# New order tables for eleven stretches of a zipformer block on one Trainium2 core

## The chip, the cores and the metric

The kernel runs on one core of a Trainium2 chip. The metric is device microseconds of one execution; the median of the runs is compared. The core has five engines that take their instructions in the order written: TensorE (PE), ScalarE (ACT), VectorE (DVE), GpSimd (POOL) and SyncE (SP, which here only issues DMAs).

## What is computed

The reference is one conformer-like block over x of shape (2, 4000, 144) in bfloat16, with 4 heads of 36:

```
x = x + 0.5 * (silu(ln(x) @ w_ff1a) @ w_ff1b)
q, k, v = heads(ln(x) @ w_qkv)
x = x + softmax(q @ k.T * 36**-0.5) @ v @ w_o
a, b = split(ln(x) @ w_pw1);  h = a * sigmoid(b)
x = x + silu(depthwise_conv5(h)) @ w_pw2
x = x + 0.5 * (silu(ln(x) @ w_ff2a) @ w_ff2b)
out = ln(x)
```

Attention is over all 4000 positions of a batch, so its exponentials (2 x 4 x 4000 x 4000) are the bulk of the work.

## The kernel before, in words

The 8000 tokens are 16 chunks of 500. A chunk goes through feed-forward 1, the projections to Q, K and V, attention, convolution and feed-forward 2; the chunks' parts overlap. Attention of one chunk runs over 63 key tiles of 64 keys, which makes 1008 *attention tiles* in all. An attention tile n is: score matmuls into two PSUM banks (`PS<-QT,KT`), an exponential into a buffer of PT, and product matmuls (`PS<-PT,VA`) that add into two PSUM banks kept for the sums. There are 11 PT buffers and 6 PSUM banks for all else.

The exponential has several forms, chosen for each tile by one letter of TYPES:

- A: ACT takes the whole tile, 128x1000, in one `ACTIVATE PT<-PS`; R is the half tile at the end of the keys.
- D: DVE makes it from bits: two `TENSOR_SCALAR PT<-PS` of 128x500 (called z0 and z1), then on PT y (`TENSOR_SCALAR`), m (`TENSOR_TENSOR`) and w (`TENSOR_SCALAR`), each 128x1000. Both m and w go into product matmuls, so that such a tile has twice as many.
- W: as D, with one z of 128x1000.

PAIRS lists attention tiles that share y, m and w as one instruction each over 2x1000 elements (`ymw_args`, L2024; `settle`, L2167).

The program is first recorded by a planner with costs (`Rec.op`, L350; `Sched`). Then `Rec.choose` (L413) puts each small flexible operation (a PSUM copy, a residual, the steps of a layernorm) on DVE, POOL or ACT by a letter of UNITS: d, p or a. `settle` rebuilds the attention tiles from TYPES, BANKS (PSUM banks of each tile) and SLOTS (PT buffers), and `Rec.arrange` (L467) orders the blocks of instructions of every engine by the table ORDER, which holds two characters for each block. The waits on semaphores are worked out after that (`finish`, L537), so the order on each engine is wholly in the tables. Every instruction is issued from one line, L591, so that groups are told apart by their tiles.

Names that the prediction uses: XN is the normalised token block of a layernorm and ST its statistics (`BN_STATS`, on DVE); RS holds the scale, made on POOL by a `TENSOR_SCALAR` and a power (`TENSOR_TENSOR`), after which four `XN<-X,RS` are written (POOL, or DVE as `XN<-X,ST,RS`) (`ln`, L1238). An SP `DMA_TRANSPOSE` then turns XN into XTB (`dma_transp`, L1216), the input of the next matmuls. The K projection is copied from PSUM into KT (`proj`, L1506). A residual (`residual`, L1360) is a DVE `SCALAR_TENSOR_TENSOR X<-PS,X`, or on ACT a copy `X<-PS`, for which PE adds x first by two matmuls `PS<-X,EYE`. U holds the convolution's input, whose edges POOL copies (`halo`, L1701).

Of the kernel before, what the change touches and what calls it, by code (L numbers as in the profile page):

```python
# [13 lines left out]
H = 4  # L14
# [38 lines left out]
        '1]1M1O1V1^1L1*1S1a1-1N1g1h1b1=141l1k#a1v1u1o1[1,1+1z1y#b2!1}1p1e1i1x1E2-2,2%1`1{1|1_21202$1w1Z1f2#2&'  # L53
        '2425#c2>232?1m1j282C2/2B1n1c1q1d#d2F29222G1s1r2Q2P2E2*2+2@262K2A2D2J2U2T2)2.2H1t2X2Y2I#e2(2^2W2]2b2['
        '2a2;2:#f272e2`2S2l2f2<2V2m2N#g2i2r3#2R2s2g2=2w2L2v2M2_2Z2h2c2O3!2d2{2z2k2j3)3*#i3-3.#j2p2q3132#h3536'
        '2y3+3/2x3:393B3A302n342|3=3>372}332o3G383H#k3K3L3,3S3?3%2u3O3P3$3;3T2t3@3I3Z3Y3F3N3M3&3<3_3^3f#l3J3C'
        '3c3[3b3g3m3l3(3Q3a3D3`3R3x3W3X3p3q#m3u3t3]3d3E4(3e3n3j3o3r4#3V4!3U3s4&473y#n#o4-4.3h3i4$3k4%414B4A3v'
        '483w4>4=#p#q#r4I4J4E4F4D4)424/4?40#s4+4,4M4N#t#u4Q4@4C4R4G4L4H4;4V4U4*4O#w#v4a4`3}4K4P494Y4e4d4:#x4h'
        '4i4<3|4T4S4Z4W4s4r454X4m4f4g3z4w4v4l4643444b3{4{4z#y#z5#4t5!5-4u4j5.4}4y4[4x4k4c4|5&52515(4]5$4q4p55'
        '56#{5=5%595:4_4o4^5D5C5>5350574n545/5X5W5<5G5+585N5M#|5F5`5;5H5Q5,5Y5Z5[5]5E5B5O5*5a5)#}5A5P5d5e5^5_'  # L60
        '5?5R5@5i5h$!5m5l$#5q5p5t5f5g6!5}5j5J5b5c5k5I5w6&6%5L5r5o5s5K5x5n5V5U6*6+5T5S5u5v$$6/6.6962$%686(636<'
        '6=$&$(6A6@6$6#6)$)6:6E6?6D656I666;6H$*61606S6R6,6C6L675z6B6W6V$+646M6F5|6Z6G6>6[6e6Y6U5{6f6X6_6-6T6K'
        '$,$-6j6i6^6m6g6]6n6N6O6J6h5y6`6P6w6x$.6q6p6{6Q6o6|6k6l6y6r7#7$$/7(7)$0$17-7,6}6b706d767!7%77$26a717&'
        '7.7;7:6v6u7>7E6z787/7D$37H7I7*7?797<7+6c7M7L$47Q7P7G7F6s6t7T7U$5$674757X7Y7]7S$77d7c7C7J7B7^7g7K7V7h'
# [2478 lines left out]
```

## Time and profile before

| | us |
|---|---|
| median of 3 runs | 866.94 (866.67 to 867.0) |
| the profiled execution | 867.84 |
| its span in the trace | 865.7 |
| PE, ACT, DVE, POOL busy | 849.3, 835.0, 835.4, 284.8 |

The span is what the trace covers; 2.14 us of the profiled execution lie outside it. The granted clock of TensorE was full but for the ends. A busy time is that of instructions in flight: one that has been issued while the one before it finishes is counted with it, so that an engine can be short of work by a little more than its idle time. The places of the change are told by the time at which their instructions run in the trace of before.

### The profile page before, as it was taken

The numbers are of one execution on the slowest core, as the hardware profiler recorded it, in microseconds if no ns is written. First come the engines' busy times: TensorE is split into PE (matmuls) and PEld (weight loads), VectorE is DVE, ScalarE is ACT, GpSimd is POOL, SyncE is SP. The second block draws the span as 40 slices with busy tenths as digits, with TensorE's granted clock in tenths as the row PEclk, the third lists the DMA queues.
The fourth block names the chain that finished last, engine by engine and source line by source line (L and its number), as shares of the span: only waits on it lengthen the run. The fifth ranks groups of instructions, "written<-read, shape, count | busy, mean of one in ns | idle before, by whom it ended". The sixth has DMA issues, their size and how long they took to land.

```text
span 865.7 us, 27015 instructions
## 1 busy us (share of the span) xinstructions
PE 849.3 (98%) x11585; PEld 411.3 (48%) x11585; DVE 835.4 (96%) x1819; ACT 835.0 (96%) x1096; POOL 284.8 (33%) x562
## 2 busy tenths in 40 slices
PE   9999999999999999999999999999999999999996
PEld 7644434444344444444444444444444544445485
DVE  7999999999999999999999999999999999999987
ACT  6999999999999999999999999999999999999975
POOL 7771331041334301432230060230550163300854
PEclk9999999999999999999999999999999999999999
DMA  3331211102113110212210020010130021100121
GB/s 102 78 58 21 33 21 36 23 14 45 34 26 51 15 27 2 40 32 45 33 38 3 2 45 3 14 32 14 27 42 11 3 57 29 29 10 14 32 53 52
DMA packets 86330, 26.90 MB, mean 31 GB/s; under 512 B 81384, under 2 KB 86210, under 8 KB 86210
## 3 DMA queue, kind: packets, MB, share of 16 engines
q1 hardware_dynamic: 84662, 24.34, 15.4%
q8 instruction: 90, 1.47, 0.7%
q10 hardware_dynamic: 1548, 0.84, 0.4%
q14 instruction: 30, 0.25, 0.1%
HBM read 3.31 MB, written 2.30 MB: 6 GB/s over the span
## 4 chain that ended last, share of the span: by engine, by line
ACT 40%; PE 40%; DVE 16%; DMA 1%; POOL 1%; issue 0%; ACTq 0%; SPq 0%; DVEq 0%; POOLq 0%
PE PS L591 40%; ACT PT L591 37%; DVE PT L591 11%; ACT TH L591 3%; DVE ST L591 1%; DVE QT L591 1%; DVE X L591 1%; POOL XN L591 1%; DVE HT L591 1%; DVE U L591 1%; DMA XTB<-XN 1%; DMA X<-in_x_dram 0%; DMA WE<-in_w_ff1a_dram 0%; DVE KT L591 0%; ACT X L591 0%
## 5 line engine op out<-in xcount | busy, mean ns | idle before, releaser
L591 ACT ACTIVATE PT<-PS 128x1000 bf16<-128x1000 f32 (+1 forms) x793 | 729.9, 1071 | 4.9 <-PE PS L591 4.1
L591 PE MATMUL PS<-QT,KT 64*64 64x500 bf16 x3968 | 460.1, 383 | 4.3 <-ACT PT L591 1.2
L591 PE MATMUL PS<-PT,VA 64*37 64x500 bf16 x4828 | 449.7, 372 | 1.3 <-DVE QT L591 0.5
L591 DVE TENSOR_SCALAR PT<-PS 128x500 int16<-128x500 f32 x425 | 279.1, 676 | 4.4 <-PE PS L591 3.1
L591 PEld LDWEIGHTS PS<-QT,KT 64*64 64x64 bf16 x3968 | 139.8, 104 | 201.7 <-ACT PT L591 99.2
L591 PEld LDWEIGHTS PS<-PT,VA 64*37 64x37 bf16 x4828 | 163.1, 96 | 105.7 <-issue 16.4
L591 POOL TENSOR_SCALAR RS<-ST 125x4 f32<-125x4 f32 (+1 forms) x132 | 31.2, 238 | 479.3 <-DVE ST L591 475.4
L591 DVE TENSOR_SCALAR PT<-PT 128x1000 uint16<-128x1000 uint16 x430 | 172.2, 418 | 1.7 <-DVE PT L591 0.2
L591 DVE TENSOR_TENSOR PT<-PT 128x1000 bf16<-128x1000 bf16 x215 | 144.4, 676 | 0.8
L591 POOL TENSOR_SCALAR XN<-X,RS 125x144 bf16<-125x144 bf16 x246 | 141.1, 587 | 3.8 <-POOL RS L591 0.5
L591 POOL TENSOR_TENSOR RS<-RS,NHALF 125x4 f32<-125x4 f32 (+2 forms) x93 | 92.4, 998 | 50.1 <-DVE RS L591 48.0
L591 ACT ACTIVATE TH<-PS 128x500 bf16<-128x500 f32 (+3 forms) x175 | 92.7, 559 | 3.8 <-PE PS L591 3.3
L591 PE MATMUL PS<-XTB,WA 72*128 72x500 bf16 (+2 forms) x280 | 71.3, 359 | 1.1 <-DMA XTB<-XN 0.4
L591 DVE SCALAR_TENSOR_TENSOR HT<-TH,PS 128x500 bf16<-128x500 bf16 (+1 forms) x120 | 71.2, 614 | 1.1 <-ACT TH L591 0.8
L591 DVE BATCH_NORM_STATS2 ST<-X 125x6 f32<-125x288 bf16 (+1 forms) x160 | 65.6, 448 | 2.2 <-DMA X<-in_x_dram 1.6
L591 DVE SCALAR_TENSOR_TENSOR X<-PS,X 125x288 bf16<-125x288 f32 x114 | 50.7, 450 | 7.2 <-PE PS L591 6.2
L591 PE MATMUL PS<-WB,HT 128*125 128x144 bf16 (+1 forms) x640 | 52.2, 229 | 0.0
L591 PEld LDWEIGHTS PS<-WB,HT 128*125 128x125 bf16 (+1 forms) x640 | 44.9, 136 | 13.5 <-issue 3.9
L591 PEld LDWEIGHTS PS<-XTB,WA 72*128 72x128 bf16 x280 | 21.5, 97 | 29.5 <-issue 8.3
L591 PE MATMUL PS<-U,DG 128*128 128x375 bf16 (+7 forms) x204 | 28.0, 263 | 0.1
L591 POOL COPY U<-U 128x2 bf16<-128x2 bf16 (+1 forms) x54 | 10.9, 236 | 42.2 <-DVE U L591 32.0
L591 ACT ACTIVATE HT<-PS 128x500 bf16<-128x500 f32 (+3 forms) x43 | 20.6, 537 | 3.4 <-PE PS L591 2.9
(98 smaller groups left out, 523.1 us busy)
## 6 DMA issues: line engine op xcount, KB each, us to landing
X<-in_x_dram SPq DMA_DIRECT2D x16, 140.6 KB
XTQ<-XTB SPq DMA_DIRECT2D x24, 70.3 KB
out_dram<-XN SPq DMA_DIRECT2D x9, 140.6 KB
XTB<-XN SPq DMA_TRANSPOSE x53, 3.8
out_dram<-PT SPq DMA_DIRECT2D x3, 140.6 KB
out_dram<-PT ACTq DMA_DIRECT2D x2, 140.6 KB
XTB<-AN SPq DMA_TRANSPOSE x15, 3.2
WA<-in_w_ff1a_dram ACTq DMA_DIRECT2D x1, 144.0 KB
```

Of the source, the lines that this page charges most:

```text
L591: ins = getattr(eng, o.name)(*o.a, **o.k)
```

## The change

Only tables change. Between the first and the last change lie ORDER for all five engines, PLACES, TYPES (3 letters), BANKS, SLOTS, UNITS (14 letters) and PAIRS (two pairs, none before). No code is touched. The change's name says that the orders in eleven narrow stretches were searched anew off the chip, with DMA landings taken a little later than their mean; nothing of that search is in the kernel.

```diff
 TYPES = (
...
-    'AAAADAAADAAAAARDAAAADAAADAAAAADAAADAAADAAAADAAADAAADAAADWAADAAADAAAAAADAAAAAARDAADAAAAAAAADAADAAAAAA'
+    'AAAADAAADAAAAARDAAAADAAADAAAAADAAADAAADAAAADAAADAAADAAADAAADAAADAAAAAADAAAAAARDAADAAAAAAAADAADAAAAAA'
...
 UNITS = (
...
-    'daddddddddddpddppdddadaadadddpddppppddppddppddddddppdppdddppaaappdadddddppppdddadddppddppddddadddppd'
+    'ddddddddddddpdddpdddadaaddddppdddpppddppddppddddddppdppdddppaaappdadddddppppdddadddppdddpddddadddppd'
...
 PAIRS = (
+    (482, 485), (787, 790),
 )
```

What the letters come to: attention tile 356 goes from W to A, 689 from W to D, 877 from D to W. Two K copies and one residual go from ACT to DVE (at 69.2, 112.6 and 320.2 us), one residual from ACT to DVE and another from DVE to ACT (422.5 and 427.2), one from DVE to ACT (622.7); the four XN of a layernorm at 626.8 go from POOL to DVE with their sign step dropped; and of the small scale steps six go from POOL to DVE and one the other way. PE has four product matmuls fewer.

On PE the order differs in nine places, at 62.6 to 124.5 us of the trace (called A below), 175.9 to 200.2 (B), 225.7 to 252.3 (C), 262.7 to 329.3 (D), 414.0 to 452.2 (E), 562.8 to 587.6 (F), 618.5 to 675.2 (G), 685.0 to 738.5 (H) and 756.3 to 786.4 (I). Some of them hold more than one of the stretches. Outside them the orders of PE, ACT and DVE are the same, those of POOL and SP differ in a few rows between them too, and the first 62 us and last 79 us are untouched.

In place A on ACT, around 68 to 118 us: PT<-PS are exponentials, and VA, QT, KT are copies of projections. Before:

```order
L591 ACTIVATE PT<-PS 128x1000 x3
L591 ACTIVATE KT<-PS 128x500
L591 ACTIVATE PT<-PS 128x1000 x2
L591 ACTIVATE TH<-PS 128x500 x2
L591 ACTIVATE PT<-PS 128x1000 x2
L591 ACTIVATE TH<-PS 128x250
L591 ACTIVATE PT<-PS 128x1000 x36
L591 ACTIVATE VA<-PS 128x14x36
L591 ACTIVATE PT<-PS 128x1000
L591 ACTIVATE QT<-PS 128x500 x2
L591 ACTIVATE PT<-PS 128x1000 x3
L591 ACTIVATE KT<-PS 128x500
```

The same place of the change:

```order
L592 ACTIVATE PT<-PS 128x1000 x5
L592 ACTIVATE TH<-PS 128x500 x2
L592 ACTIVATE PT<-PS 128x1000 x2
L592 ACTIVATE TH<-PS 128x250
L592 ACTIVATE PT<-PS 128x1000 x36
L592 ACTIVATE VA<-PS 128x14x36
L592 ACTIVATE PT<-PS 128x1000
L592 ACTIVATE QT<-PS 128x500 x2
L592 ACTIVATE PT<-PS 128x1000 x15
```

Both KT copies are gone from ACT, and the exponentials on both sides of each follow each other. DVE does the copies as `CAST KT<-PS`.

In place E on DVE, around 425 to 432 us, with attention tiles 482 and 485. Before:

```order
L591 TENSOR_SCALAR PT<-PS 128x500 x4
L591 TENSOR_SCALAR PT<-PT 128x1000
L591 CAST VA<-PS 128x2x36
L591 TENSOR_SCALAR PT<-PT 128x1000
L591 SCALAR_TENSOR_TENSOR X<-PS,X 125x288
L591 TENSOR_TENSOR PT<-PT 128x1000
L591 CAST KT<-PS 128x500
L591 TENSOR_TENSOR PT<-PT 128x1000
L591 CAST VA<-PS 128x14x36
L591 TENSOR_SCALAR PT<-PT 128x1000
L591 CAST KT<-PS 128x500
L591 TENSOR_SCALAR PT<-PT 128x1000
```

The same place of the change:

```order
L592 TENSOR_SCALAR PT<-PS 128x500 x4
L592 TENSOR_SCALAR PT<-PT 128x2x1000
L592 CAST VA<-PS 128x2x36
L592 TENSOR_TENSOR PT<-PT 128x2x1000
L592 BN_STATS ST<-X 125x6 x2
L592 CAST KT<-PS 128x500
L592 CAST VA<-PS 128x14x36
L592 TENSOR_SCALAR PT<-PT 128x2x1000
L592 CAST KT<-PS 128x500
```

The four z stand as they did; the six instructions behind them have become three. The other pair (787, 790, at 658 to 663 us) is made likewise.

In place G on DVE, around 631 to 637 us; the `BN_STATS` make the statistics of the layernorm whose transposed output is awaited at 649 us. Before:

```order
L591 TENSOR_TENSOR PT<-PT 128x1000
L591 TENSOR_SCALAR PT<-PS 128x500
L591 RECIPROCAL RD<-PS 125x8
L591 TENSOR_SCALAR PT<-PT 128x1000
L591 TENSOR_TENSOR AN<-PS,RD 125x4x72
L591 TENSOR_SCALAR PT<-PT 128x1000
L591 BN_STATS ST<-X 125x6 x2
```

The same place of the change:

```order
L592 TENSOR_TENSOR PT<-PT 128x1000
L592 BN_STATS ST<-X 125x6 x2
L592 RECIPROCAL RD<-PS 125x8
L592 TENSOR_SCALAR PT<-PT 128x1000
L592 TENSOR_TENSOR AN<-PS,RD 125x4x72
L592 TENSOR_SCALAR PT<-PS 128x500
```

The statistics have moved ahead of five instructions. On POOL the two edge copies of U that stood behind the first scale step of this layernorm now stand ahead of it, and its power stands ahead of the four XN of another layernorm instead of behind them.

More of the change, by code (lines that the diff above doesn't have):

```diff
@@ new lines @@
+        '9@9?9D9C9990$D9G9H9897939:9/9,9R9Q9F9E$E9U9V9A9B9K9J9&9(9Y9Z$F9^9_9S9%9L9+9$949c9b9T9W9X9f9[9l9m$G9p'
+        '9q9e9d$H9I9u9t9g9<9=9o:#9;9]:!9n9x9>:&:($I9P9a:+:$9y:,9M:):6:%:5:*9`:/9i9j9k9O:::9:0:.9h$J:>:=9v:7:A'
+        ':B:8:-$K9w:E:L:<:K9N9|9r:F:?:O9z:P:D:;9s9}:S:T9{:4:W:N:3:_:^$L:C:X:Q:2:c:b:U:@:`:J:a:1:f:g:M:j:V:p:q'
+        ':e$M:t:u:G:H:d:k:R:[:y:x:I:]:s:r:|:Z;(;&$N;+;,:}:v:h;0;/$O;:;9:Y:o:i;=:{:z;>:n;B;A:m;-;1;3;.;2;;$P;K'
+        ';L:w;O;?;@:l;P;E;*;%;C;4;$;T;S;);D;F;<;X;W$Q$R;N;U;[;V;];Y;`;M;Q;a;5;R$S;Z;6;d;k;7;#;j;G;J;!;H;o;I;n'
@@ new lines @@
+        ';e;c;b$T;r;s;^;m;q;l;v;w$U;z;{;p;_<&<!<#$V<*;i;h<+;x;8<5<4;y<0<1;t$W$X<?<><(<)<9<8<B<C;};|;f<%<$;u<F'
+        '<G;g$Y<K<J$Z$[$]$^$_<N<O<R<A<2<S<=<6<3<@<I<H<L<M<.<7<V<W<,</<<<-<E<Z<_<[$`<e<f<Q<X<`<T<D<Y<j<i$a<^<]'
+        '<t<s<U<m$b<w<x<l<k<P<h<n<:<|<{$c=#=$$d<a<b=(=)<u<y<z=!=0=-=,=&<}<g=1<v=6=7=%=+$e=:=;<;=J$f=?=>$g$h$i'
+        '=C=8=B===9=4=/=<=3=2=G<q=K=F<c=5<r<d=*=Q=P=@=a=E=D=A=T=U$j=Y=X<o=b=S=H=I=R=]=^$k=g=h=V=W=[=w<p=.=k=l'
+        '$l=o=p=Z=x=O=N=i=j=s=t$m>!=}=q=r=L=M>&>%$o$n>*>+=_={=f>#>/>8>$>.=d=v=u=`=c>5>4=e=n>?>(>->>$p=m=|>C>B'
@@ new lines @@
+        '>9$q>F>G>A=z>@=y>)>K>J$s>,>7>N>O$r>Y>X$t>^>]>S>L>2>3>6>Q>a>b>R>I>=>P>H>1>e>f$v$u>j>D>i>E>[>m>;>Z>s>t'
+        '><>`>_>h>c>d>M>x>w$w>n>k>{>:>|>v>g>0>z?$>u>U?#>l>V$x$y>}?0?(?)?%>y?!$z?,>W?5${?6>q?<?;?*?+?&?/>p>T??'
+        '?@>o>r?.?-?D?C?G?N?M?R?A?B?Q$|?U?V?H?4?3?>?=?T?E?a?`?Y?P?O?e?d$}?W?i?h?F?b?Z?S?:?7?8?9?c?l?X?r?s%!%#'
+        '?v?w?j?k?m?z?{?f%$@!@#%%?u?x@(?t@&?y@+?g@1?_@2@$%&?K@,?^?L@6@5?1@*@:@)?2?|@?@@@9?}@4?]@3@C@D?[@K@8@%'
+        '@H@G%(@7?J@R@Q@F?I@L@E@U@V@I@/?q@^@0@J?p@Y@Z%)@W@e@_@d@.@S@-@A@X@T@h?n@i%*@[@]@l@m@v@g@<@;@f@B@w@p@O'
@@ new lines @@
+        '@P?o@kA&@{@z@>@n%+A!A#@=@o@y@xA-@q@MA.@b@}@|A(@c@jA2A1%,%-A/A0A;A<A@A?%.%/A3A4A%AI@rAJ%0%1ANAM@sA$A='
+        '@NAQARAC@aA>AK%2AVAUAPAA@`A5AZAY@uAOADA*@tA_A^A6A+ASABA)ATA,AbAcA[%3%5%6AgAfAWAL%4AjAk%7A]AnAoA9AeAd'
+        'AsAr%8AaAvA:A`A}A|A7AX%9B$B%%:B*B)AlB.ApAqAtA8B-Aw%;B1B2AmAEAHAGAFB8B5B!AuBBB#B>B?B3B9%<B+BCB,B/AxB4'
+        'AzAiBGBKBFAyB(AhBJB0BQBPB7B6A{B&BUBTBXBY%=BDBdBcBEBSBRBAB]BIBgBVBhB<B=BWB@BHB^BrBqBkB[B;BOBuBvB:BfBi'
+        'BjBlBZBzBy%>C(C)BwBNBxBsBtC,C-B}BeBMB_C0C1%?C4C5BLC?C.B|B{C!C>C+C2C*C8C3CBCCC7BaBmBnCFBbCG%@CQCPC9C@'
@@ new lines @@
+        'CAC6C#C$CTCUCICJC/CKCYCXC&BoBpCaCHC]C^CRCbB`CVCWCDChCg%A%BCkClC%CEC_C[CfCSCoCpCe%CCOCZCtCsCnCmCiC|Cx'
+        'CwCNC{C<C=D%D&%E%DCLCdCqD+CMD.CvD*C`CyD/CuD)D(CcCrC}CjD#C;D2CzD9D8C:D3D,D<D=DFD1D-D0D$DAD@%FDLDMD!D:'
+        'DGD>D?DPDQ%GDTDUDND;DODRDSD_D`DXDcDdDV%HDhDgDYDBDbDaDlDk%IDWDuDvDoDCD6DDDfD7DzDeDHD5DEDyE%D4DIE!D}%J'
+        'DiD|E&E,E-DjDmE#E1DwDnE0E$%KE5E4DxDpDJD{E.DKE9E8D[DZD^E2%LE<E=E(E)E*E+D]E3EDE6E@%MEJE;EIE?DsDtECE7E>'
+        'ENEMDrE:E/EYEQEREBEADqEZEUEV%N%OEaE`%P%Q%RELEdEeEOEGEHEXEiESEhETEWEFEbElEKEPErEsEmEgEEEcEfEwEv%SE{Ez'
@@ new lines @@
+        'F&EuE]EjEtE_F#F!%TF-F.EkE|E^F(F2F1EyF$%WF6F5EoE[F9E}ExFCF:%U%VFDEpF0EnFMEqFJFIF4F8F3F%FUFNF=F;F<F/F,'
+        'FQFRF7F>FKFLF*F+F]F[%[%X%YFPFSFaF`FdFeFOFH%ZFAFTF)FmFhFiFVFcFGF_F^FrFsFbFBFlFwFvFEFFG#FgFfFjF{FzF?Fk'
+        'G!Fu%]G&F@G-G.FpF}G(FtFyFxG1G2%_%^G5G6G$FqFYFoG:G9F|G=G%G0FnG+GCGDG7G>FZG3GPGHGGG;G8G)GOG4GKGLG<G^G,'
+        'FWG*G/GVGUG_GEFXGIGZGJGY%`%a%bGkGdGNGjGXGAGTGWGoGSGnG]GeGrGsGBGlGMGmGFG}G|GvG[GwGQH$H%%c%dH/GRG?H0Gp'
+        'H4H3GuH#GtH&GaH(GbGcH)G`G@H8H7H*H1GqH!H2H;H<%eGzH@H?G{H9H6H:H5HCHD%fGyH=HGHHGxGiH>HeHKHUHEHTHFGgHAH-'
@@ L160 @@
-        '$h$x$k$l$u$p$v%%$|$}%!$y${$o$z%#%$%&%(%)%+%*%5%,%-%6%.%/%0%1%2%3%7%8%4%:%;%9%<'
+        '!!!$!#!%!(!)!*!+!,!-!&!.!/!2!0!1!4!9!3!:!;!5!6!7!8%;!<%<%=%>%@%?%A!=!>!?!@!A!B!C!D!E!H!G!F!I!J!P!K!R'
+        '!L!M!N!O!V!W!T!Y!Q!S%B!U![!]!Z!X%C%D%E%F%G%H%I!^!_%J%K%L%M%N%O!`!a%P!b%Q%R!c%S%T%V!d%U%X%W%Y%Z!e!f%['
+        '%]!g%^%_%`%a%b%c%d%e%f%g%h%i%j%k%l%m%n%o%p%q%r%s%t%u%v%w%x%y%z%{%|%}&!&#&$&%!h&&!i!j&(&)&*&+&,&-&.&/'
+        '&0&1&2&3&4&5&7&6&8&9&:!k!l&;&<&=!m&>&?&@&A&B&C!n&D&E!o&F&G&H!p&I&J&K&L&M&N&O!q&P&Q&R&S&T&U&V&W&X&Y&Z'
@@ L161 @@
+        '$B.N.O.P$C.Q.R$D.S.T.U.V$E.W$F.X.Y.Z.[.].^._.`$G.a.b.c.d$H.e.f.g.h.i$J.j$I.k.l.m.n.o.p$M.q.r.t$K$N$L'
+        '.u.s.v.y.{.z.|.w/$/!.}/#$P$O/*/%/&/)/(.x$R$T$o$V$Q$X$Y$Z$[$p$]$k$_$`$l$b$^$d$e$g$S$U$W$q$u$r$a$c$h$f'
+        '$v$i$j$s$n$t%#$z${$|$w$y$m$x$}%!%$%%%&%)%(%3%*%+%4%,%-%.%/%0%1%5%6%2%8%9%7%:'
     ),
@@ new lines @@
+    ')!+!($-!,!)!*!#,&!+!-!*!!!%)-!(!$!!!+#&!-!(!!!*!,$)!+$&!%!-!,#*!(!!*)!#!*!-#)!%!&!(!$!+!(%)!%!,!+!*!'
+    '!!)!$!*%,!&!!!,!)!#!-!$(+!)!!!)!+-$!(!&#,!*!%!,%$!+!(!(-!!-!*!+*$!)!&!!!,!)!&!-#$!+!!!)%(!*!,!&!!!#!'
+    '*&-!+!(!,+)!!!$!#(-!+!%!!#&!*#$!&%-,%!)!+!(!$!)!*!$&+!(!-!),#!*!!!%!!-+!#!*!(!%*)!&)+!(%$!,!!!-!#!*!'
+    '+!#!-,,!&!$!!!*)(!%!#!%!&!%*#!(!)!$-+!,!)!&(%!+!,!#!)!*,+!$!!%(!)!#!-!+!&!,%(!)!$(-!#!&!*&)!+!,!-!%)'
+    '!!,!-!#!+$,!!!*!(%#!,!-!#!&!!!!#+!-!$!,!%))!*!(!*--!,!&!#!!!,&$!+!(!!-%!$!)!$)#!%!&!#!(-,!*!+!%&)!!!'
@@ new lines @@
+    '-!%!)#+!*!%!-!$!,!(!&!-!,#%!&!$!*!+!-#&!!!(!$%%!)!!!+!*(,!#!)!-%!!+!(!*+)!$!#!&!,!+!(!)+*!#!$!!!*!,!'
+    '+!)!$!#(%!-!&*!!#!(!$!)!-!,#*-+!%!&!(!)!!(%!&!$!#!%&&!,!(,+*)!!!$-*!-!#!)!)(&!%!!$#!,!+!&,-!*!,!%!#!'
+    '+!(-$!#&*!,!+!%!)!,!*!+($!!!%!)!,!&%!!!%(!,!-!*!+()!#!,!)#*!-!$!&!(*%!*!$!-!-)!!,!%!&!!)#!,!+!%!*-,!'
+    '(!)!$,+!#!%!(!&!#!)(+!%!-!,#&!%!*!$!+#!!)!-!($&!*!!!%!#&)!-!%!+!-)!!$!,!&!%*(!#!+!!!),&!$!#!&!+%(!!!'
+    '*!)$&!$,%!-!!!+#%!*!-!(!,!,#%!*!!!$!%!$!&!+!#!*!&-)!(!%)+!!!,##!$!#+*!!!-!*+$!(!+!%!!!%!#!,$&!)!*!%!'
```

318 lines of the change are left out of this document (136 added, 182 removed).

## The prediction

> **What bounds the kernel now.** First the page: span, busy time by engine, and the chain of work that ended last.
>
> ```profile
> span 865.7 us, 27015 instructions
> PE 849.3 (98%) x11585; PEld 411.3 (48%) x11585; DVE 835.4 (96%) x1819; ACT 835.0 (96%) x1096; POOL 284.8 (33%) x562
> ACT 40%; PE 40%; DVE 16%; DMA 1%; POOL 1%; issue 0%; ACTq 0%; SPq 0%; DVEq 0%; POOLq 0%
> ```
>
> Three engines are busy at 96% or more, and the chain changes hands between them. So no single engine's work sets the end; a stretch becomes shorter only if the engine that holds the chain there gets less to do or waits less, and the other two can follow. The second view is the table by windows, for the nine places A to I (columns: stretch, its length, then busy time and instructions of PE, weight loads, DVE, ACT and POOL).
>
> ```profile
> 62.60:124.50 61.90, 61.27 (x917) 26.86 (x918) 59.14 (x129) 61.21 (x75) 19.21 (x33) 1.00 0.17 26
> 175.90:200.20 24.30, 23.69 (x317) 10.10 (x316) 23.76 (x47) 24.30 (x31) 7.96 (x13) 1.00 0.17 33
> 225.70:252.30 26.60, 26.55 (x346) 10.76 (x336) 26.15 (x55) 26.57 (x34) 5.43 (x10) 1.00 0.14 27
> 262.70:329.30 66.60, 65.85 (x947) 28.89 (x943) 65.93 (x137) 66.10 (x81) 15.90 (x36) 1.00 0.20 30
> 414.00:452.20 38.20, 37.75 (x538) 17.07 (x530) 37.77 (x80) 37.77 (x47) 12.57 (x33) 1.00 0.20 28
> 562.80:587.60 24.80, 24.52 (x316) 10.47 (x311) 24.64 (x49) 24.21 (x32) 6.76 (x12) 1.00 0.13 28
> 618.50:675.20 56.70, 55.58 (x750) 25.26 (x740) 56.05 (x116) 55.29 (x72) 21.54 (x44) 1.00 0.20 30
> 685.00:738.50 53.50, 52.82 (x717) 24.66 (x709) 52.46 (x113) 52.92 (x68) 25.52 (x52) 1.00 0.19 39
> 756.30:786.40 30.10, 29.62 (x406) 13.60 (x400) 28.92 (x60) 30.10 (x40) 1.17 (x4) 1.00 0.05 10
> ```
>
> Length less busy time is an engine's idle time. ACT's is 0.69 in A, 0.50 in D, 1.41 in G and 4.23 us over all nine; PE's is 0.63, 0.75, 1.12 and 5.05. That is the size of the prize: a few us out of 866, wherever a reorder puts its instructions. The whole work hardly changes (one exponential more and two K copies fewer on ACT, one attention tile fewer on DVE), so that almost all of any gain must come out of such idle time. That makes the answer small from the start.
>
> **A, the two K copies.** The chain in order of time (start, length, what) runs through both copies, with five of its pieces:
>
> ```profile
> 68.27 0.98 ACT PT L591
> 69.26 0.48 ACT KT L591
> ...
> 105.14 5.43 PE PS L591 x77
> ...
> 112.58 0.59 ACT KT L591
> 113.16 13.93 ACT PT L591 x16
> ```
>
> The first copy lies in a run of ACT that lasts to 105.14; taken off ACT it gives up to 0.48 us. The second comes after DVE's part of the same bank, and ACT stands still before it. These are PE's scores and ACT at that point:
>
> ```profile
> 112.24 0.38 PE L591 MATMUL PS<-QT,KT 64*64 64x500 bf16 x4
> 112.58 0.59 ACT L591 ACTIVATE KT<-PS 128x500 bf16<-128x500 f32 x1 [0.67 <-DVE KL L591]
> 113.06 2.79 ACT L591 ACTIVATE PT<-PS 128x1000 bf16<-128x1000 f32 x3
> ```
>
> Without the copy the next exponential needs only its scores, at 112.24 + 0.38 = 112.62 instead of 113.06 where the copy let it go: 0.44 us, and not the whole idle 0.67 and the copy's 0.48 (113.06 - 112.58), because PE is late there. Together 0.92 us at most. PE must come forward by as much, and its idle time in A is 0.63, so I take 0.6; the low end is 0, where PE's order does not let the scores come sooner. DVE pays for two copies. Two that stand in line show the price of one:
>
> ```profile
> 428.14 0.67 DVE L591 CAST KT<-PS 128x500 bf16<-128x500 f32 x1
> 428.73 0.66 DVE L591 TENSOR_TENSOR PT<-PT 128x1000 bf16<-128x1000 bf16 x1
> ```
>
> From start to start that is 0.59, so 1.18 us of DVE for both, beside 61.90 - 59.14 = 2.76 us of its idle time in A. That idle time is the cover; if it does not lie at the copies, up to 1.18 us comes back on the PSUM banks that PE waits for.
>
> **G, the statistics moved ahead.** PE's first matmul behind the landing, then the chain's piece of the DMA, then DVE and POOL ahead of it:
>
> ```profile
> 648.97 0.60 PE L591 MATMUL PS<-XTB,WA 72*128 72x500 bf16 x2 [0.40 <-DMA XTB<-XN]
> 644.49 4.44 DMA XTB<-XN
> 635.31 0.19 DVE L591 RECIPROCAL RD<-PS 125x8 f32<-125x8 f32 x1
> 636.40 0.81 DVE L591 BATCH_NORM_STATS2 ST<-X 125x6 f32<-125x288 bf16 x2
> 637.43 0.31 POOL L591 COPY U<-U 128x2 bf16<-128x2 bf16 x2
> 638.03 3.53 POOL L591 TENSOR_SCALAR XN<-X,RS 125x144 bf16<-125x144 bf16 x4
> 642.66 1.80 POOL L591 TENSOR_SCALAR XN<-X,RS 125x144 bf16<-125x144 bf16 x4
> ```
>
> Statistics, scale, eight XN and a DMA of 4.44 us feed a matmul for which PE waits 0.40. The statistics move ahead of five instructions, z among them, so to about one z (0.6 as it stands in line) before 635.31; that is up to 636.40 - 634.7 = 1.7 us. The four XN that DVE takes over stand ahead of them and cost back. Their nearest row is the last of these four, by form (count, busy, mean ns, idle):
>
> ```profile
> L591 DVE TENSOR_SCALAR PT<-PS 128x500 int16<-128x500 f32 x420 | 273.1, 670 | 4.4 <-PE PS L591 3.1
> L591 DVE TENSOR_SCALAR PT<-PS 128x1000 int16<-128x1000 f32 x5 | 6.0, 1193 | 0.1
> L591 DVE TENSOR_SCALAR PT<-PT 128x1000 uint16<-128x1000 uint16 x430 | 172.2, 418 | 1.7 <-DVE PT L591 0.2 <-PE PS L591 0.2
> L591 DVE TENSOR_SCALAR PT<-X,ST,RS 125x144 bf16<-125x144 bf16 x20 | 5.1, 318 | 0.0
> ```
>
> 5.1 / 20 = 0.26 us each, about 1.0 for four. The copies of U gone from this place save 0.31 more. The net is 1.7 - 1.0 + 0.3 = 1.0 us earlier, which is more than the 0.40 that PE waits, so I take the whole 0.4 away; behind it PE's own order is next. The ends are 0.4 gained and, if those XN push the statistics back instead, 1.0 lost (DVE has 56.70 - 56.05 = 0.65 us of idle time in G to hide them).
>
> **D, tile 356 to ACT and a residual to DVE.** PE at 320, ACT at 320, and the chain:
>
> ```profile
> 320.22 0.29 PE L591 MATMUL PS<-X,EYE 125*125 125x144 bf16 x2
> 320.44 0.41 PE L591 MATMUL PS<-QT,KT 64*64 64x500 bf16 x4
> 320.55 0.41 ACT L591 ACTIVATE X<-PS 125x288 bf16<-125x288 f32 x1 [0.39 <-PE PS L591]
> 320.89 2.80 ACT L591 ACTIVATE PT<-PS 128x1000 bf16<-128x1000 f32 x3
> 319.21 14.33 PE PS L591 x190
> ```
>
> PE holds the chain from 319.21 on, and loses the two EYE matmuls (320.44 - 320.22 = 0.22) and four product matmuls, about as much again: 0.43 at most. ACT gains an exponential (2.80 / 3 = 0.93) and loses the residual (0.34) and the 0.39 of idle time before it, so it would be 0.2 longer if it set the end. Between 0.43 gained and 0.2 lost I take 0.2 gained: the chain is PE's, but ACT's 0.50 of idle time in D does not cover the added 0.59 fully.
>
> **E and G, the paired tiles.** The chain in E has these as the first and the last of 48 pieces, all on DVE but for waits of issue:
>
> ```profile
> 409.52 3.67 DVE PT L591 x8
> ...
> 441.35 0.59 DVE PT L591
> ```
>
> No row shows an instruction of 2x1000. The nearest are z of 500 and of 1000 columns above: twice 670 less 1193 leaves 147 ns, an estimate of what joining two saves; in line, where ends overlap, the saving is less, so between 0 and 0.15 us for each of three joins. Against it, tile 482's m waits for both y: one y, 0.42 us by its row above, is the loss at the other end. I take 0.2 gained for the pair in E, where the chain from 409 to 442 us is DVE's, and nothing for the other, where ACT holds it.
>
> **The rest is order alone** (B, C, F, H, I, and what moves in A, D, E, G beside the above). F and H exchange a pair of z for one wide z and back, 0.147 each way. B and I have no ACT idle time at all and C 0.03, so I give these three nothing. F and H have 0.59 and 0.58, E 0.43: I take 0.2 of the 1.6 together, with 1.6 at one end and the same lost at the other, since an order can as well put a wait where none was.
>
> **Sum.** 0.6 + 0.4 + 0.2 + 0.2 + 0.2 = 1.6 us off the profiled execution, 867.84 - 1.6 = 866.2 (span 864.1, with the same 2.14 around it). That execution was 0.90 above the median of the runs, 866.94; on the median's scale the forecast is **865.3**. A measurement of this kernel can tell about 0.2%, 1.7 us, from no change: the forecast lies at that line.
>
> **A rule that speaks against the pairs and for the XN on DVE.** The row first: four XN on POOL took 3.53 us at 638.03 and 1.80 at 642.66, with the same shapes. The Trainium skill, "SBUF — State Buffer", section "Who interferes with whom", says that a VectorE instruction in a two-port performance mode and a GpSimd instruction exclude each other for the whole length of one. By that rule a paired y or w shuts POOL out for longer at a time; the sum above would lose what the last rival below loses. The two rows agree with some such exclusion, but do not show which DVE instruction did it.
>
> **Rivals.**
> - *Given back.* Each stretch saves on the engine that holds the chain, and the next piece of the chain lies on another that was not early. For it: in A PE holds 5.43 us at 105.14 between two runs of ACT. Then nothing is left, 866.9. Against: the order behind every stretch is unchanged, and an engine that waited on the early one moves with it.
> - *All of it stays.* A gives 0.92, D 0.43, order half of its 1.6 and the rest as above: 0.92 + 0.4 + 0.43 + 0.2 + 0.8 = 2.75, or 864.2. For it: ACT's and PE's idle time is larger than that. Against: A alone exceeds PE's 0.63.
> - *Slower: DVE becomes the bound.* It gets 1.18 in A and 1.0 in G where the chain is ACT's, PE's and POOL's. If its gaps lie elsewhere, both reach the end through PSUM banks released late: 2.2 us, 869.1. It decides from the point at which the gaps at those places are shorter than what is added; G's 0.65 against 1.0 speaks for it, A's 2.76 against 1.18 against it.
> - *POOL shut out by the pairs.* Two pairs, two long instructions each, a y's 0.42 us longer: 1.7 us for the layernorms behind. 865.3 + 1.7 = 867.0. For it: 3.53 against 1.80. Against: POOL is busy 12.57 of 38.20 us in E, so that most of its lateness is absorbed.
>
> **How the numbers follow.** Forecast 0.52, given back 0.15, all stays 0.15, slower 0.13, POOL 0.05. With about half of the open terms at one end the forecast lies between 864.0 and 866.7, about half of it beyond the line at 865.2. Faster: 0.15 + 0.25 = 0.40. Slower: 0.13, of which a case that is only half as bad would still be within the line, so 0.12. Within 0.2%: the rest, 0.48. The range that leaves out the slow case and a little at the low end is 863.6 to 867.5; it holds the single worst end of order alone on both sides (865.3 + 0.2 + 1.6 = 867.1, and 865.3 - 1.4 = 863.9).
>
> **What would show it.** In A, ACT's exponentials around 112 us follow each other with an idle time of at most 0.3, and DVE has `CAST KT` there with no PE wait on it. In G, the wait of PE on DMA at 649 is gone, and the landing comes about 1 us sooner behind the matmuls ahead of it. In D, PE's chain is some 0.4 shorter. The paired y takes well under twice 418 ns. The forecast is wrong if the places A to I end together less than 0.3 us or more than 3 us earlier, or if new waits of PE on DVE's copies show in A.

## The result and the profile after

The changed kernel takes 868.7 us (median, 868.26 to 869.02) beside 867.0 for the kernel before in the same place (866.67 to 868.0). The ratio is 1.0019, 95% interval 1.0012 to 1.0026: 1.7 us slower (1.0 to 2.3), where 1.6 us faster was forecast. Its profiled execution took 868.67 us, with a span of 866.5. Span, busy time and chain:

```profile
span 866.5 us, 27005 instructions
PE 849.2 (98%) x11581; PEld 410.3 (47%) x11581; DVE 835.8 (96%) x1820; ACT 836.1 (96%) x1095; POOL 288.3 (33%) x552
PE 43%; ACT 42%; DVE 14%; DMA 0%; issue 0%; POOL 0%; DVEq 0%
```

The busy times of PE, DVE and ACT moved by 1.1 us at most (ACT, 835.0 to 836.1). So the page alone does not say where 1.7 us went, and neither does the chain's split.

A finer measure does. The exponential of an attention tile on ACT is the same instruction in two programs, so the time between the starts of two such exponentials can be compared stretch by stretch. The kernel before was profiled a second time (e17 below, 867.33 us), and all stretches are set against that execution. Each number is the stretch's length less that of e17, in us; the stretches are named by the times of before.

| | to 60 | 60-78 | 78-107 | 107-130 | 225-262 | 262-335 | 410-470 | 618-676 | 684-740 | all, to 820 |
|---|---|---|---|---|---|---|---|---|---|---|
| before, first profile | 0.27 | -0.11 | 0.00 | -0.10 | 0.00 | -0.15 | -0.28 | 0.54 | 0.01 | 0.31 |
| changed | -0.07 | 0.52 | 0.62 | -0.34 | 0.20 | 0.24 | -0.10 | 0.01 | 0.16 | 1.10 |
| changed, again (e13) | 0.04 | 0.53 | 0.62 | -0.35 | 0.16 | 0.25 | 0.03 | 0.01 | 0.18 | 1.30 |
| e1, all but A | -0.18 | -0.02 | 0.00 | -0.08 | 0.19 | 0.21 | -0.11 | 0.00 | 0.16 | 0.00 |
| e9, A with copy 1 on ACT | -0.09 | 0.25 | 0.65 | -0.33 | 0.00 | -0.03 | 0.13 | -0.02 | -0.04 | 0.38 |
| e6, copy 1 alone | -0.08 | 0.97 | -0.03 | -0.15 | 0.00 | -0.18 | -0.05 | -0.01 | -0.02 | 0.44 |
| e5, copy 2 alone | -0.46 | -0.02 | 0.00 | 0.09 | 0.00 | -0.17 | 0.04 | -0.02 | -0.02 | -0.56 |
| e10, C alone | -0.21 | -0.02 | 0.00 | 0.25 | 0.18 | -0.19 | -0.49 | -0.02 | -0.04 | -0.56 |
| e11, D alone | -0.32 | -0.02 | 0.00 | -0.29 | 0.00 | 0.21 | -0.32 | -0.03 | -0.03 | -0.83 |
| e12, tile 356 alone | -0.47 | 0.01 | 0.00 | -0.12 | 0.00 | 0.16 | 0.33 | 0.02 | 0.01 | -0.05 |
| e3, end of G alone | -0.11 | -0.02 | 0.00 | -0.08 | 0.00 | -0.12 | -0.07 | 0.49 | -0.02 | 0.03 |
| e18, one memset back | -0.04 | 0.40 | 0.61 | -0.35 | 0.19 | 0.26 | -0.09 | 0.02 | 0.16 | 0.93 |

The stretches that are left out differ by 0.17 or less. Where two programs have the same order, most stretches repeat within 0.03 us. Those that do not are the start; 107-130 (-0.29 to 0.25 with that place unchanged); 262-335, by one exponential at 282.8 us; 410-470, by one at 427.8; and 618-676, 0.54 longer in the first profile of before alone. (At 60-78 that profile is 0.11 shorter; the last section says why.) So a place's loss can be read from one trace, but the total of one trace is uncertain by half a us. Against e1, where A is as before, the changed kernel loses 0.80 us from 60 to 225 us, in **A**. **C** costs 0.2, **D** 0.37 (0.24, and 0.13 more, since the exponential at 282.8 came early), H 0.16; G and E come out at about nothing, and I gives 0.1 back. That is about 1.4 us together, inside the 1.0 to 2.3 of the times.

In A the chain shows who was late. In e17 ACT holds it from 68.12 to 104.94 us without a gap (start, length, what):

```profile
58.86 9.26 PE PS L591 x135
68.12 0.98 ACT PT L591
69.10 0.48 ACT KT L591
69.58 1.79 ACT PT L591 x2
...
74.44 30.50 ACT PT L591 x34
104.94 0.04 issue
```

In the changed kernel it runs over DVE, K copies among its pieces (copy 1 is the one at 69.76), and then stays on PE for 16 us:

```profile
63.13 0.60 DVE KT L592
...
67.99 1.76 DVE PT L592 x3
69.76 0.58 DVE KT L592
70.34 1.83 DVE PT L592 x4
72.17 0.59 DVE KT L592
```

```profile
78.81 0.60 DVE QT L592
79.41 0.04 issue
79.46 16.25 PE PS L592 x241
95.70 0.02 issue
95.72 6.43 ACT PT L592 x7
```

The copy of 0.48 us is gone from ACT, but ACT stands still for 0.98 at two points where in e17 it does not (start, length, instruction, idle time before it):

```profile
64.22 1.90 ACT L592 ACTIVATE PT<-PS 128x1000 bf16<-128x1000 f32 x2 [0.35 <-PE PS L592]
...
69.94 1.90 ACT L592 ACTIVATE PT<-PS 128x1000 bf16<-128x1000 f32 x2 [0.63 <-PE PS L592]
```

The cover of DVE was not there. Rows of e17's table by windows (stretch, length, busy of PE, weight loads, DVE, ACT, POOL):

```profile
60.00:78.00 18.00, 18.00 (x249) 7.26 (x248) 17.88 (x36) 17.86 (x25) 4.51 (x7) 1.00 0.20 39
78.00:107.00 29.00, 28.94 (x452) 13.62 (x452) 27.43 (x55) 29.00 (x35) 8.02 (x13) 1.00 0.13 25
107.00:130.00 23.00, 21.82 (x290) 8.42 (x292) 21.52 (x54) 22.23 (x29) 6.90 (x14) 1.00 0.12 19
```

DVE's idle time in A lies behind 78 us (1.57 and 1.48); at the first copy it has 0.12 of 18.00.

### The profile page after: what moved, and what is told of

It reads as the page before. It is cut to its first block, busy times and chain, and to the rows that moved or that the text cites. A ratio compares the mean times of both kernels' runs of the same rounds, so it can differ in the third digit from the quotient of the medians.

```text
span 866.5 us, 27005 instructions
## 1 busy us (share of the span) xinstructions
PE 849.2 (98%) x11581; PEld 410.3 (47%) x11581; DVE 835.8 (96%) x1820; ACT 836.1 (96%) x1095; POOL 288.3 (33%) x552
## 4 chain that ended last, share of the span: by engine, by line
PE 43%; ACT 42%; DVE 14%; DMA 0%; issue 0%; POOL 0%; DVEq 0%
PE PS L592 43%; ACT PT L592 38%; DVE PT L592 10%; ACT TH L592 3%; DVE HT L592 1%; DVE ST L592 1%; DVE QT L592 1%; DVE U L592 1%; DMA X<-in_x_dram 0%; DVE X L592 0%; DVE KT L592 0%; ACT X L592 0%; POOL RS L592 0%; DVE VA L592 0%; DVE SW L592 0%
## 5 line engine op out<-in xcount | busy, mean ns | idle before, releaser
L592 POOL TENSOR_SCALAR RS<-ST 125x4 f32<-125x4 f32 (+2 forms) x126 | 31.4, 250 | 473.2 <-DVE ST L592 461.3
L592 POOL TENSOR_SCALAR XN<-X,RS 125x144 bf16<-125x144 bf16 x242 | 144.0, 608 | 3.4 <-POOL RS L592 0.5
```

The costliest lines, as they stand in the source:

```text
L592: ins = getattr(eng, o.name)(*o.a, **o.k)
```

## The experiments

### Which place loses

**e1**: the changed kernel with place A as before.

```diff
-place A as changed
+place A as before
```

> The change with place A (62.6 to 124.5 us, both K copies and the orders around them) set back to the kernel before; all other places as changed. Theory 1 (the loss is made in A: the exponentials of the change are 1.0 us later behind A than ahead of it, beside before): 1.0 us faster than the change, about 867.7. Rival (the loss is spread over D and E, 0.35 and 0.3 us later each, and A's 1.0 is an accident of the one profiled execution of before): within 0.3 us of the change, 868.4 to 869.0.

867.51 us beside 866.77, ratio 1.0008 (0.9999 to 1.0017). With A undone some 0.7 us of loss is left, so A costs about 1.0 of 1.7.

**e2**, **e4** and **e7**: the kernel before with half of A changed: 60 to 78 us (e2), 78 to 146 us (e4), and the first half with copy 1 left on ACT (e7).

```diff
 A up to 78 us           e2: +changed   e7: +changed, copy 1 on ACT
 A from 78 us on         e4: +changed
```

> The kernel before with only the first part of A changed (62.6 to 78.3 us: the first K copy from ACT to DVE, a scale step from DVE to POOL, and the order there). Theory 1 in its form 'VectorE becomes the bound in the first part of A': slower than before by 0.4 to 0.7 us, and the chain of work runs through DVE pieces between 62 and 79 us. Rival (ACT's gain of 0.48 us from the copy stands and the loss is made behind 78 us): 0.3 to 0.5 us faster than before.

> The kernel before with only the rest of A changed (78.4 to 124.5 us: the second K copy from ACT to DVE, two scale steps from POOL to DVE, and the order there). Theory 1: the part loses 0.6 us up to 105 us because PE's order holds the scores back, gains up to 0.7 at the copy and loses 0.5 behind it, 0.3 to 0.5 us slower in sum. Rival (the copy's gain stands, and only the first part of A loses): 0.2 to 0.4 us faster than before.

> The kernel with the first part of A alone (62.6 to 78.3 us), as run before, but its K copy put back on ACT: the order of the change without the copy's move. Theory (the copy on a full DVE is the loss): within 0.3 us of the kernel before, so 1.0 us faster than the same with the copy on DVE. Rival (the order is the loss): 0.8 us or more slower than before, as with the copy on DVE.

868.11 and 867.97 beside 866.77: 1.0013 (1.0004 to 1.0022) and 1.0011 (1.0002 to 1.0020). e7: 868.27 beside 866.93, 1.0017 (1.0008 to 1.0026). Either half costs as much as the whole, and the copy's place made no difference. But these kernels change PT buffers in the middle of A; e2 and e7 lose 1.0 us at 82 to 85 us, where their order is that of before. That may be the cut, so nothing is built on what they do behind 78 us. e9 has no such cut.

**e3** and **e8**: the kernel before with G changed from 644 us on; e8 without its pair of tiles.

```diff
 PAIRS = (
+    (787, 790),      e3; left out in e8
 )
```

> The kernel before with only the second part of G changed (644.8 to 675.2 us: order, PT buffers and the pair 787, 790). In the profiled executions the exponentials came forward by 0.58 us over this part. Theory 1 (places act by themselves, and what one gains stays to the end): 0.6 us faster than before, 866.4. Rival (the gain there only takes back a lateness that the change itself had brought along from earlier places, or the pair costs): within 0.2 us of before.

> The kernel with the second part of G alone (644.8 to 675.2 us), as run before (0.56 us slower than before), but with the pair 787, 790 split again into y, m and w for each tile, in the place of the joint ones. Theory (joined instructions save DVE some time, and the order is the loss): 0.5 to 1.0 us slower than before. Rival (the pair is the loss, since tile 787's m waits for both tiles and POOL is shut out for longer): within 0.2 us of before.

867.33 beside 866.77, 1.0005 (0.9996 to 1.0014), and 867.73 beside 866.93, 1.0007 (0.9998 to 1.0016). The traces tell more: 618 to 676 us is 0.49 longer in e3 and 0.70 in e8, while all of G together costs nothing. The end of G loses without its beginning, and the pair saves 0.2 there.

### The two K copies

**e5** moves copy 2 alone, **e6** copy 1 alone; the order is that of before. For e6:

```diff
-L591 ACTIVATE KT<-PS 128x500
+L591 CAST KT<-PS 128x500
```

> The kernel before with one thing changed: the K copy at 112.6 us goes from ACT to DVE, behind the second z of attention tile 88; no order is touched. Theory (the copy's move was worth what the prediction said, and the orders around it lost more): the exponential behind it comes 0.5 to 0.75 us sooner and the kernel is 0.4 to 0.7 us faster than before, about 866.2. Rival (a copy on DVE always comes back through the PSUM banks that PE waits for): within 0.2 us of before or slower.

> The kernel before with one thing changed: the K copy at 69.2 us goes from ACT to DVE, behind the first wide-tile z of attention tile 32; no order is touched. Theory (DVE has only 0.11 us of idle time between 62 and 78 us, so its 0.59 us come back on the path): 0.3 to 1.0 us slower than before, with the chain on DVE up to 78 us. Rival (ACT's 0.48 us is gained, and only the order of the first part of A lost): 0.2 to 0.5 us faster.

e5: 866.91 beside 866.93, 1.0002 (0.9993 to 1.0012). By its trace beside e17's, the exponential behind the copy starts 0.63 us sooner and the next six give 0.28 and 0.41 back: nothing is left. e6: 867.83, 1.0010 (1.0001 to 1.0019). Here ACT waits twice behind the place of the copy:

```profile
69.36 1.00 ACT L591 ACTIVATE PT<-PS 128x1000 bf16<-128x1000 f32 x1 [0.35 <-PE PS L591]
70.88 1.00 ACT L591 ACTIVATE PT<-PS 128x1000 bf16<-128x1000 f32 x1 [0.51 <-PE PS L591]
```

0.97 us lost at 60 to 78 us, and kept. PE, which makes the scores for these exponentials, waits for the copy on DVE, which has no gap there:

```profile
70.42 0.41 PE L591 MATMUL PS<-QT,KT 64*64 64x500 bf16 x4 [0.68 <-DVE KT L591]
```

**e9**: all of A changed, but copy 1 on ACT.

```diff
+place A as changed, but at 69 us
-CAST KT<-PS 128x500
+ACTIVATE KT<-PS 128x500
```

> The kernel before with the whole of place A changed, PT buffers included, but with the first K copy (69.2 us) left on ACT, where it stood. Theory (DVE was full at 62 to 78 us and cannot take that copy): the loss of place A, about 1.0 us, goes nearly all; the exponentials from 60 to 130 us take the time that they take before, within 0.3 us, and the total is within 0.4 us of before. Rival (the new order in A is what costs, with or without the copy): A still loses 0.6 us or more between 60 and 130 us, and the total stays about 0.7 to 1.0 us above before.

867.63 beside 866.81, 1.0012 (1.0003 to 1.0021). My theory falls: 0.25 and 0.65 us are lost in the first two stretches with the copy where it was. The new **order** (with its PT buffers and scale steps) costs 0.9 there, of which some 0.35 comes back behind 107 us, where copy 2 has moved too (0.25 and 0.10 against e1, the first no more than that stretch's own spread).

The changed kernel loses 0.27 more at 60 to 78 us (0.52 against 0.25), but not by copy 1. It loses 0.47 at the exponential at 63.9 us, ahead of the copy, where e9 loses 0.06; at the copy it loses 0.27, and e9 0.42 less 0.08 just behind it. e2 and e7 differ in that copy alone, and this stretch lies ahead of their cut: 0.21 with the copy on DVE (e2), 0.27 with it on ACT (e7). So in the new order the copy's place does not matter here. What makes the 0.47 is the subject of e13 and e18.

### C and D

**e10** changes C alone, **e11** D alone, **e12** only the types: tile 356 to ACT and its residual to DVE, in the order of before. On ACT, for e12:

```diff
-L591 ACTIVATE PT<-PS 128x1000 x2
-L591 ACTIVATE X<-PS 125x288
-L591 ACTIVATE PT<-PS 128x1000 x5
+L591 ACTIVATE PT<-PS 128x1000 x8
```

> The kernel before with place C alone changed. The changed kernel lost 0.25 us at 255 to 262 us, just behind C and ahead of D. Theory (C's order shows its price behind its end): the stretch from 255 to 262 us is 0.25 us longer here too, the total 0.2 to 0.3 us above before. Rival (D's first rows cost it): nothing moves here, 0.0 within 0.05 us in every stretch from 201 to 335 us.

> The kernel before with place D alone changed: its order, tile 356 on ACT and its residual on DVE. Theory (ACT becomes the full engine in D, busy in all of it): 262 to 335 us takes 0.3 to 0.5 us more than before, total 0.3 to 0.5 us above. Rival (the loss seen in D was brought in from the places ahead): within 0.1 us of before in that stretch. The prediction's own step would be 0.2 us less.

> The kernel before, in its own order, with one thing of place D: attention tile 356 goes from DVE to ACT, and its residual from ACT to DVE. The prediction's step: PE loses 0.43 us of work and 0.2 us is gained, at most 0.43. Theory now (ACT is full there, and gets 0.93 for the 0.34 it gives and its 0.39 of waiting): 0.1 to 0.3 us lost between 262 and 335 us. Rival (the retyping gains as predicted, and the new order around it loses more): 0.2 to 0.4 us gained here, so that the order alone costs 0.6 to 0.8.

e10: 866.84 beside 866.81, 1.0003 (0.9994 to 1.0011); in its trace C costs 0.18, of it 0.25 at one exponential at 256.9 us, behind C's last changed row. That size is below what the times can tell. e11: 867.64, 1.0013 (1.0004 to 1.0022); these 0.83 us are more than its trace shows, but the interval begins at 0.35. e12: 867.17, 1.0005 (0.9996 to 1.0014). In the traces e11 loses 0.34 and e12 0.02 us, once the exponential at 282.8 is set aside. So the theory of a full ACT was wrong as a price: the added exponential just fills what ACT gives up. Rows of e17 and e12 at that point:

```profile
318.03 2.22 ACT L591 ACTIVATE PT<-PS 128x1000 bf16<-128x1000 f32 x2
320.64 0.41 ACT L591 ACTIVATE X<-PS 125x288 bf16<-125x288 f32 x1 [0.39 <-PE PS L591]
320.99 4.59 ACT L591 ACTIVATE PT<-PS 128x1000 bf16<-128x1000 f32 x5
```

```profile
317.58 7.60 ACT L591 ACTIVATE PT<-PS 128x1000 bf16<-128x1000 f32 x8
```

In e17 the five behind the residual start 2.96 us after the two ahead of it; in e12, 3.00. In e11 the same place is shorter (0.08 more, 0.32 less, then 0.13 more), but 0.24 at 271 to 276 us and 0.23 at 291 to 304 us are lost ahead of it, where only order changed.

### What in A's order loses

**e13**: the changed kernel once more, with no edit.

> The changed kernel itself, profiled a second time. In its first profile one y at 60.8 us took 0.83 us instead of 0.42, beside a memset of POOL, and PE waited 0.41 us at 63.8 us for the copy behind it; with the same order in place A that y took 0.42 us in two other programs. Theory (that long y is an accident of this one execution): here it takes 0.42 us, and 60 to 78 us is 0.2 to 0.4 us longer than before instead of 0.63; the rest of place A is as in the first profile. Rival (the change makes it): 0.83 us again, and 0.6 us.

868.08 beside 866.62, 1.0019 (1.0009 to 1.0028). The long y stands in both profiles, with all of A the same within 0.02 us. So it is no accident of one execution. But the order of place A does not make it alone: in e2, e7, e9, e14, e15 and e16, which have the memset in the same row, the y takes 0.42 to 0.43.

**e14** and **e15**: e9 with pieces of DVE's order put back, e14 at 70.0 to 78.5 us, e15 two more at 62.6 to 65.4 and 80.2 to 84.8; **e16**: e9 with PE's order at 108.3 to 124.5 us put back.

```diff
-DVE's rows at 70.0 to 78.5 us as changed    (e15: three pieces; e16: PE's rows at 108.3 to 124.5)
+the same rows in the order of before
```

> As e9 (place A changed, first K copy left on ACT), but with DVE's rows at 70.0 to 78.5 us in the order of before. Theory (DVE's new order there hands the scores' banks back late at 72 to 79 us, PE falls behind and holds the chain to 95 us): the 0.65 us lost at 78 to 107 us shrinks to 0.3 or less. Rival (PE's own new order loses it): still 0.5 us or more.

> As e14, with two more short pieces of DVE's order put back, at 62.6 to 65.4 and at 80.2 to 84.8 us. Theory: as e14, and the 0.28 us lost at 60 to 78 us shrinks too, by about 0.1 us. Rival (PE's order): no less than in e9, and possibly more, since PE then hands over in an order that DVE does not follow.

> As e9, but with PE's rows at 108.3 to 124.5 us in the order of before. Score and product matmuls of 64x500 run up to four at a time, each on a quarter of the array, and the new order there sets more of them behind one of the same quarter. Theory (that costs PE time which the chain pays): 107 to 130 us becomes 0.3 to 1.0 us shorter than in e9. Rival (ACT sets the time there, PE has room): the same within 0.1 us, and the gain of the second K copy stays whatever PE's order is.

871.63, 870.88 and 870.88 beside 866.62: 1.0058 (1.0043 to 1.0073), 1.0049 (1.0032 to 1.0065), 1.0049 (1.0033 to 1.0066). None gave anything back; each lost 3.0 to 4.2 us more than e9 at its place. One wait does it in e14, on PE:

```profile
75.17 0.81 PE L591 MATMUL PS<-PT,VA 64*37 64x500 bf16 x10 [2.46 <-DVE PT L591]
```

The orders of PE and DVE fit each other; one of them alone is worse than either pair. So these runs do not tell whose order loses the 0.65 us at 78 to 107 us (0.79 and 0.90 in e14 and e15), and e16 does not price PE's packing.

**e17**: the kernel before, profiled again. **e18**: the changed kernel with one POOL row put back.

```diff
-MEMSET XN 128x1024
 TENSOR_SCALAR RS<-ST 125x4
 TENSOR_TENSOR RS<-RS,NHALF 125x4
 TENSOR_SCALAR XN<-X,RS 125x2x72 x4
+MEMSET XN 128x1024
```

> The kernel before itself, profiled a second time. Its first profile was 0.9 us above the median of its runs. Theory (that execution had two late DMA landings, one ahead of 20 us and the one of 4.44 us at 644 us): here the start comes 0.2 to 0.7 us sooner, the landing at 644 us takes some 0.4 us less, PE's wait of 0.40 us behind it is smaller or gone, and all else repeats within 0.1 us. Rival (it is how this program runs): 4.44 us and the wait of 0.40 us again. Its time against before is 1.000 either way.

> The changed kernel with one POOL row put back: the memset of XN that place A moved ahead, to 60.4 us, stands behind the four XN again, as before. Theory (that memset keeps the y beside it on DVE waiting, 0.83 us instead of 0.42, and PE waits for the copy behind it): the y takes 0.42 us, PE's wait of 0.41 us at 63.8 us goes, and 60 to 78 us is 0.25 to 0.4 us shorter than in the changed kernel, the total likewise. Rival (DVE is late there for another reason): the y still takes 0.8 us, and no more than 0.1 us is gained.

e17: 867.18 beside 867.27, 1.0000 (0.9991 to 1.0009). PE's matmuls behind the landing in G do not wait; the landing had been late once:

```profile
648.69 0.60 PE L591 MATMUL PS<-XTB,WA 72*128 72x500 bf16 x2
```

e18: 868.51, 1.0014 (1.0005 to 1.0023). The y and the memset in the changed kernel, then in e9, then the y in e18:

```profile
60.81 0.83 DVE L592 TENSOR_SCALAR PT<-PT 128x1000 uint16<-128x1000 uint16 x1
```

```profile
60.41 0.95 POOL L592 MEMSET XN<- 128x1024 bf16 x1
```

```profile
60.88 0.42 DVE L591 TENSOR_SCALAR PT<-PT 128x1000 uint16<-128x1000 uint16 x1
```

```profile
60.08 0.94 POOL L591 MEMSET XN<- 128x1024 bf16 x1
```

```profile
60.95 0.41 DVE L593 TENSOR_SCALAR PT<-PT 128x1000 uint16<-128x1000 uint16 x1
```

In e18 the y takes 0.41, and the step at the exponential at 63.8 us is 0.31 smaller, as expected. Of it 0.12 is lost at 60.5 us, where the two programs came out of another meeting of DVE and POOL differently (the last section), and 0.07 at 69: 60 to 78 us is 0.12 shorter, not 0.25. That other meeting is a rival that e18 leaves untested: it came out in e18 as it did in e9, where the y is short with the memset in the changed kernel's row. In the changed kernel the memset still runs 0.55 us when the y starts, in e9 0.14. So the long y goes with a memset that comes late beside it, and e18 does not tell how much of that is the memset's row and how much the meeting at 57 us.

The Trainium skill, "SBUF — State Buffer", section "Who interferes with whom", says that of a VectorE instruction in a two-port mode and a GpSimd instruction the one that issues second waits for the whole of the other. The trace agrees with a hold of about that kind: the y took 0.42 longer where the memset still ran 0.55, and nothing where it ran 0.14, as if the memset let go some 0.14 us ahead of the end of its row. It shows no port.

## Why the prediction was wrong

- **The step that failed: "The rest is order alone ... I take 0.2 of the 1.6 together".** Instead of gaining 0.2, order cost about 1.1 us: 0.55 in A (0.25 and 0.65 lost, 0.35 got back with copy 2's move among it; e9), 0.2 in C, 0.3 in D (e11 less e12), 0.16 in H, with 0.1 back in I. The long y beside the memset that A's order moved ahead adds 0.27. These 1.4 are nearly all of the 1.7. They lie inside the ends of 1.6 that the prediction gave to order, but with the wrong sign; and the range had no room for the other gains failing beside it. The error was to count ACT's and PE's idle time as a prize. Before, ACT held the chain in A for 37 us without a gap, so that a new order had nothing to gain there and could only put a wait in.
- **A, the copies (-0.6): wrong.** Copy 2 did what was said (0.63 sooner in e5, 0.44 forecast), and it was given back within 5 us, which is the first rival. In the changed kernel the wait before that exponential is still 0.58, not 0.3 or less:

```profile
113.26 1.00 ACT L592 ACTIVATE PT<-PS 128x1000 bf16<-128x1000 f32 x1 [0.58 <-PE PS L592]
```

  Copy 1 fell on a DVE with 0.12 us of room. The 2.76 us of cover were an average over 62 us; that was the point from which the rival "DVE becomes the bound" was to decide, read over the wrong stretch. Alone the copy costs 0.97. In the new order its move costs nothing that shows (e2 against e7), and gains nothing either. That rival named the time best (869.1), but by luck: the loss came of the order. Whether the order had to lose that to make room for the copy is not shown.
- **G, the statistics (-0.4): the mechanism right, the gain not there.** They stand 1.7 us sooner on the clock of before (636.01 below, less 1.3 us by which all is late there, against 636.40). But the 4.44 us landing and PE's wait of 0.40 belonged to one execution. It was also part of the 0.90 by which that execution stood above the median, and so was counted twice. PE waits in the changed kernel all the same, for DVE (its row, then that of the statistics):

```profile
650.07 0.58 PE L592 MATMUL PS<-XTB,WA 72*128 72x500 bf16 x2 [0.32 <-DVE PT L592]
```

```profile
636.01 0.81 DVE L592 BATCH_NORM_STATS2 ST<-X 125x6 f32<-125x288 bf16 x2
```

- **D, tile 356 (-0.2): the wait of 0.39 went, the gain did not come.** Alone the retyping is worth 0.0 (e12), inside the ends -0.43 and +0.2. What D lost is order.
- **The pairs (-0.2): the price right.** By the changed kernel's rows a joined y or w saves 2 x 416 - 686 = 146 ns (147 was estimated), a joined m 2 x 684 - 1185 = 183:

```profile
L592 DVE TENSOR_SCALAR PT<-PT 128x1000 uint16<-128x1000 uint16 x420 | 168.3, 416 | 1.8 <-PE PS L592 0.2
L592 DVE TENSOR_TENSOR PT<-PT 128x1000 bf16<-128x1000 bf16 x210 | 142.9, 684 | 1.0
L592 DVE TENSOR_SCALAR PT<-PT 128x2000 uint16<-128x2000 uint16 x4 | 2.7, 686 | 0.0
L592 DVE TENSOR_TENSOR PT<-PT 128x2000 bf16<-128x2000 bf16 x2 | 2.4, 1185 | 0.0
```

  The pair in G saves 0.2 (e3 against e8), for which nothing was taken. In E no gain shows beyond that stretch's own spread. No loss of the kind that the rival on POOL names shows in G, where the pair was tested alone; in E it was not.

Open stays whether PE's or DVE's order loses the 0.65 us at 78 to 107 us, which way the meeting at 57 us goes in most executions of the changed kernel, and what sets the exponentials at 282.8 and 427.8 us, which move from one execution to the next. No kernel tried beat the one before; e5 and e10 equal it.

## What to carry to other kernels

Where an engine holds the chain without a gap, look for cover in windows of the length of the edit, not in the share of a whole place; and a new order there is a risk, not a prize. Profile the kernel before twice before a wait of 0.4 us is put into a sum. With fixed orders, the starts of the same instruction in two traces place a loss of 0.1 us that the times cannot tell.

## What the runs showed that was not expected

- With the same order, most stretches repeat within 0.03 us between executions and chips; the spread of the times sits at a few points (up to 0.7 us at the start, 0.54 in G).
- DVE and POOL meet at 57 us in one of two ways. In e17 POOL's XN starts at 57.03 and DVE's m there takes 0.82 us; in the changed kernel XN starts at 57.27, half a us behind the scale step ahead of it, and m takes 0.68:

```profile
57.31 0.82 DVE L591 TENSOR_TENSOR PT<-PT 128x1000 bf16<-128x1000 bf16 x1
```

```profile
57.23 0.68 DVE L592 TENSOR_TENSOR PT<-PT 128x1000 bf16<-128x1000 bf16 x1
```

  The order up to there is the same in all programs. Both profiles of the changed kernel and the first of before went the second way, all others the first. The second way gives 0.11 us back at 60.7 us; but with A's order the memset of XN comes 0.33 us later by it (60.41, against 60.08 in e9), and so meets the y at 60.8.
- Putting one engine's order back within one place costs 3.0 to 4.2 us, about twice the 1.7 of the whole change or more.
